# Seven block products over pairs of f tiles for the first matmul of the MLP, in the last two units

## The chip, the cores and the metric

The kernel runs on one core of one Trainium2 chip. The metric is the device time of one execution in microseconds (us). Five engines work side by side, each through its own queue in program order: TensorE (PE in the profile, its weight loads PEld), VectorE (DVE), ScalarE (ACT), GpSimd (POOL), and SyncE (SP), whose queue issues the DMA transfers. They meet through semaphores only. Matmuls write to PSUM, eight banks of 512 fp32 columns in each of 128 partitions; all else lies in SBUF or in DRAM.

## The reference

Two layers of each of two kinds in turn, on 2048 tokens of 1024 channels, in fp32: A, a gated long convolution on the normalized input, and B, an MLP with a squared ReLU.

```
x = x + A(layernorm(x)); x = x + B(layernorm(x)); x = x + A(layernorm(x)); x = x + B(layernorm(x))
B(x): h = x @ w1 + b1            # 1024 -> 3584
      h = max(h, 0) ** 2
      out = h @ w2 + b2          # 3584 -> 1024
```

Both layers of a kind use the same weights, and the convolution of A doesn't depend on x (only its gate does).

## The kernel before

**Units.** The MLP is computed for 512 tokens at a time: two layers of four blocks make eight units, run one after the other in the order of ORDER. What the convolution needs is computed beside units 0 to 4 on GpSimd and VectorE. Before a unit, its tokens are gated, normalized, turned on TensorE (transposes) and split into two tiles xh and xl.

**Three matmuls for one.** Every fp32 product is three matmuls on halves, hi x hi, hi x lo and lo x hi (mm3, lines 338 to 340): a number is cast to a shorter form by ScalarE (the high half), and what is left is the low half, a subtraction on VectorE. This holds for weights (line 1015 the cast, line 1023 the low half, in w_hi and w_lo) and for activations (1562, 1567).

**The first matmul (m1).** An f tile is 128 of the 3584 inner channels of the MLP; there are 28. For each f tile and each half kh of the 1024 input channels stands one step: a weight tile of 128 x 512 (four 128 x 128 blocks) against 512 tokens, 4 x 3 = 12 matmuls of 512 columns, gathered in one PSUM bank. Then relu_w makes the squared ReLU (lines 1559, 1560), splits it, and for the second tile of a pair forms four sums of blocks (1572 to 1575) and splits these as well (1579, 1583).

**The second matmul (w2) in the last three units.** Units 5, 6 and 7 (WINO) compute it as seven block products for eight, over pairs of f tiles, halves of the tokens and halves of the output columns. WORD gives the order of the seven blocks, WSUM where each is added. A step is one block of one pair: 2 x 3 = 6 matmuls of 512 columns. The 14 pairs are taken in four chunks, WCH = (3, 3, 4, 4): first all m1 steps of the chunk, then all its w2 steps, block by block, after which evict_w (line 1593) adds two PSUM banks to the accumulators.

**Weights.** All steps stand in one list, and each has a weight with a number in the same order. w_advance, called at each step, does three things ahead of the step: it loads raw weights up to 8 ahead (W_LOAD; w_load, lines 1004 and 1007, into a ring of 8 rows called wr), makes high halves up to 4 ahead (W_HI) and low halves up to 3 ahead (W_LO). Split pairs lie in a ring of six buffers (whl). Some weights are stored split at their first use (w_store) and later loaded as a pair of 512 KB, with no work on chip (split_kept, from_pair, line 1013); for the sums of w2's blocks ("t"), those are the weights of pairs 10 and up with a < 2, which are blocks 4 and 5. Everything is issued in one program order: an engine may run ahead of the step at which an instruction was issued, as far as data and buffers allow, but never past an earlier instruction in its own queue.

**What happens at a unit's start.** At its fifth step load_acc (line 1716) loads the four accumulators, at the seventh load_b2 (1721) loads the bias b2, at the eleventh add_b2 (1725) adds it on GpSimd:

```
b2_at = (7, 11) if u in WINO else (12, 16)
lag.at(b2_at[0], load_b2, bst)
lag.at(b2_at[1], add_b2, bst, accs)
```

lag is a list of things due so many steps later; it is emptied at the beginning of a step, ahead of w_advance. The block results of the unit before are stored by store_w (line 1600), on the same SP queue.

**Preparation.** In unit 5 and 6, prep_w readies the next unit from 90 steps before the end: early combines and takes statistics, late normalizes (847), turns (856) and splits (862, 864) one tile of 128 tokens after the other.

## Time and profile before

| | |
|---|---|
| median of 3 runs | 2715.45 us (2715.27 to 2721.26) |
| the profiled execution | 2718.27 us, its span 2716.5 us |
| mean granted TensorE clock | 0.996 |
| PE busy | 98% of the span |
| DVE, ACT, POOL busy | 73%, 41%, 31% of the span |
| unit 6, unit 7 from their first matmul | at 2125.25 and 2419.63 us |

A group line gives source line, engine, operation, tiles (out<-in), shapes, count, then busy us and mean ns of one, then the idle time of the engine just before, and what ended it. A timeline line gives start, duration, engine, line, operation, tiles and count, and in brackets the idle time before it and what released it. A line of a table by stretches gives the stretch and its length, then busy us and instructions of PE, PEld, DVE, ACT and POOL, the granted TensorE clock, the share of the DMA engines, and GB/s. Ends of matmuls are modelled, and matmuls overlap, so a pitch is read from starts.

### The profile page before, as it was taken

The page shows a single profiled execution, that of the slowest core. Times are in us where ns is not written, and L with a number is a line of the kernel's source. Part 1 is how long each engine was busy: PE and PEld are TensorE (multiplying, and loading weights), DVE is VectorE, ACT ScalarE, POOL GpSimd, SP SyncE. Part 2 cuts the span into 40 slices and gives each one's busy share as a digit, 9 for nine tenths or more (in the row PEclk, how much of TensorE's full clock was granted, in tenths as well). Part 3 has the DMA queues.
Part 4 walks back from the last instruction along what each step waited for, and adds up shares of the span by engine and source line. Part 5 has one row for each costly group of instructions (what it writes and reads, how often), then busy time and mean ns, then how long its engine had stood idle before and what let it go on. Part 6 is the DMA issues. An engine that isn't in the chain of part 4 may idle for free.

```text
span 2716.5 us, 36547 instructions
## 1 busy us (share of the span) xinstructions
PE 2660.4 (98%) x12568; PEld 2227.2 (82%) x12568; DVE 1984.6 (73%) x3042; ACT 1114.5 (41%) x1912; POOL 848.3 (31%) x520
## 2 busy tenths in 40 slices
PE   8999899999999999999999999999999999999998
PEld 7888787888888888888888888887888788878887
DVE  7878888788987878778677655367786666656554
ACT  4354344434444323442234322244455544444443
POOL 2336565445532745236552554001000100000000
PEclk9999999999999999999999999999999999999999
DMA  8889898689999898888977786798888766685555
GB/s 260 266 299 316 279 312 291 224 308 381 327 299 332 297 339 276 284 327 292 352 262 269 285 322 221 256 306 292 303 288 309 259 213 225 208 311 182 171 178 194
DMA packets 375898, 755.05 MB, mean 278 GB/s; under 512 B 43792, under 2 KB 159136, under 8 KB 375712
## 3 DMA queue, kind: packets, MB, share of 16 engines
q1 hardware_dynamic: 375712, 752.72, 80.9%
q8 instruction: 99, 1.62, 0.2%
q14 instruction: 87, 0.71, 0.1%
HBM read 602.63 MB, written 149.95 MB: 277 GB/s over the span
## 4 chain that ended last, share of the span: by engine, by line
PE 80%; DVE 7%; DMA 7%; issue 2%; POOL 2%; ACT 1%; SPq 1%; DVEq 0%; POOLq 0%; ACTq 0%
PE p L339 24%; PE p L340 24%; PE p L338 24%; PE p L1099 2%; DVE whl L1023 1%; DMA wr<-w 1%; DMA cg<-gd 1%; DMA whl<-wd_t 1%; PE pt L338 1%; PE pt L340 1%; PE pt L339 1%; POOL cp L528 1%; DVE sm L532 1%; DMA whl<-wd_m 1%; DMA yt<-yd 0%
## 5 line engine op out<-in xcount | busy, mean ns | idle before, releaser
L528 POOL TENSOR_TENSOR cp<-cx,cg 128x384 f32<-128x384 f32 (+5 forms) x288 | 545.2, 1906 | 567.5 <-DVE sm L532 376.6
L338 PE MATMUL p<-xh,whl 128*128 128x512 f32 (+1 forms) x1840 | 706.6, 384 | 0.6 <-DMA whl<-wd_m 0.6
L340 PE MATMUL p<-xh,whl 128*128 128x512 f32 (+1 forms) x1840 | 703.1, 382 | 0.8 <-POOL whl L1023 0.8
L339 PE MATMUL p<-xl,whl 128*128 128x512 f32 (+1 forms) x1840 | 703.1, 382 | 0.1
L1015 ACT CAST whl<-wr 128x512 fp32r<-128x512 f32 x637 | 385.4, 619 | 456.2 <-PE p L340 321.6
L1023 DVE TENSOR_TENSOR whl<-wr,whl 128x512 fp32r<-128x512 f32 x622 | 499.9, 826 | 71.2 <-ACT whl L1015 65.7
L338 PE MATMUL p<-whl,rh 128*128 128x512 f32 x1372 | 541.6, 395 | 4.2 <-ACT whl L1015 2.4
L339 PE MATMUL p<-whl,rh 128*128 128x512 f32 x1372 | 537.5, 392 | 5.5 <-DVE whl L1023 4.6
L340 PE MATMUL p<-whl,rl 128*128 128x512 f32 x1372 | 536.6, 391 | 0.0
L340 PEld LDWEIGHTS p<-xh,whl 128*128 128x128 f32 x1840 | 346.2, 188 | 68.4 <-POOL whl L1023 1.0
L338 PEld LDWEIGHTS p<-xh,whl 128*128 128x128 f32 x1840 | 346.6, 188 | 66.4 <-issue 1.1
L339 PEld LDWEIGHTS p<-xl,whl 128*128 128x128 f32 x1840 | 346.4, 188 | 65.8 <-DVE xl L1412 0.3
L1725 POOL TENSOR_TENSOR acc<-acc,px 128x1024 f32<-128x1024 f32 x32 | 84.8, 2681 | 738.2 <-DMA wr<-w 568.5
L339 PEld LDWEIGHTS p<-whl,rh 128*128 128x128 f32 x1372 | 259.0, 189 | 60.5 <-DVE whl L1023 7.5
L338 PEld LDWEIGHTS p<-whl,rh 128*128 128x128 f32 x1372 | 259.1, 189 | 58.1 <-ACT whl L1015 3.1
L340 PEld LDWEIGHTS p<-whl,rl 128*128 128x128 f32 x1372 | 258.9, 189 | 54.3
L1506 DVE TENSOR_TENSOR rl<-wr,rh 128x512 fp32r<-128x512 f32 x140 | 138.5, 990 | 183.7 <-ACT rh L1501 183.5
L532 DVE TENSOR_REDUCE sm<-cp 128x128 f32<-128x384 f32 (+5 forms) x288 | 249.5, 874 | 12.1 <-POOL cp L528 12.1
L1498 ACT ACTIVATE wr<-p,b1t 128x512 f32<-128x512 f32 x138 | 95.3, 690 | 367.2 <-PE p L340 366.4
L1567 DVE TENSOR_TENSOR rl<-wr,rh 128x256 fp32r<-128x256 f32 x84 | 51.0, 607 | 195.8 <-ACT rh L1562 195.6
L1593 DVE TENSOR_TENSOR acc<-p,acc 128x512 f32<-128x512 f32 x168 | 111.7, 687 | 67.7 <-PE p L340 67.6
L1605 DVE TENSOR_TENSOR acc<-p,acc 128x512 f32<-128x512 f32 x152 | 99.8, 686 | 82.2 <-PE p L340 82.2
(263 smaller groups left out, 3176.8 us busy)
## 6 DMA issues: line engine op xcount, KB each, us to landing
whl<-wd_m SPq DMA_DIRECT2D x379, 512.0 KB, 5.4
wr<-w SPq DMA_DIRECT2D x493, 256.0 KB, 5.3
wr<-td SPq DMA_DIRECT2D x152, 256.0 KB, 4.1
wd_m<-whl SPq DMA_DIRECT2D x70, 512.0 KB, 6.1
cx<-xd SPq DMA_DIRECT2D x48, 512.0 KB, 6.0
cg<-gd SPq DMA_DIRECT2D x48, 512.0 KB, 6.6
gd<-fg SPq DMA_DIRECT2D x72, 256.0 KB, 6.3
cx<-xd SPq DMA_DIRECT2D x48, 384.0 KB, 5.9
```

What stands on the lines that cost most here:

```text
L338: PE.matmul(o, lh, rh, start=start, stop=False, skip_group_check=skip)
L339: PE.matmul(o, lh, rl, start=False, stop=False, skip_group_check=skip)
L340: PE.matmul(o, ll, rh, start=False, stop=stop, skip_group_check=skip)
L528: G.tensor_mul(pr.rearrange("p c i -> p i c"), xt[:, 0:j + 1], gt[:, j::-1])
L532: V.tensor_reduce(sm[:, ty, jj], st["pr"], axis=AX.X, op=OP.add)
L1015: A.copy(t[:, 0], raws[n]["t"])
L1023: ENG[e[n % len(e)]].tensor_sub(t[:, 1], raws[n]["t"], t[:, 0].bitcast(F32))
L1498: A.activation(r, st["o"], AF.Relu, bias=b1t[:, st["f"]:st["f"] + 1])
L1506: V.tensor_sub(st["lo"], st["r"]["t"], st["hi"].bitcast(F32))
L1593: V.tensor_add(a, os[n], a)
L1605: V.tensor_add(accs[tt][:, d], o, accs[tt][:, d])
L1725: G.tensor_add(a, a, st["t"])
```

## The change

In units 6 and 7 (M1W) the first matmul is computed as seven block products instead of eight, too. For a pair of f tiles, the weight is cut into four blocks a11, a12, a21, a22 (second index: the half of the 1024 input channels; first index: the f tile), each 128 x 512, and the tokens into b11 to b22 (halves of input channels, halves of tokens). Sums of the weight blocks s1 to s4 are formed on GpSimd, in place or in rows of the ring (sums_a, sums_b), and sums of the token blocks once per unit in prep_w (first, second). Each product is a step "s1" of its own: 4 x 3 = 12 matmuls of 256 columns. Products are added up in two PSUM banks per pair; in between, m1_out copies a partial result out or across (three copies on ScalarE) and adds two on VectorE. The seven products of a pair are numbered like the blocks: 5, 1, 3, 2, 6 (with the first f tile then complete), 7, 4 (the second).

Beside it: the low halves of the products 3, 4 and 7 go to GpSimd; none of the product weights is kept split in DRAM; the order of the products of two pairs is interleaved, with the last two w2 steps of the chunk before and the first four of this one put in between; the chunks of units 6 and 7 are (2, 4, 4, 4); of the kept sums of w2's weights, blocks 5 and 6 are kept instead of 4 and 5; one square of the activation goes to another buffer (yt); two convolution tiles (sm, fk) become larger so that token pieces can lie in them; and the scratch for dynamic DMA is set to 1024.

```diff
+M1W = (6, 7)
+M1_KEY = {5: "s1", 1: "a11", 3: "s4", 2: "a12", 6: "s2", 4: "a22", 7: "s3"}
+M1_LO_G = (3, 4, 7)
-WCH = (3, 3, 4, 4)
+WCH, WCH_M1 = (3, 3, 4, 4), (2, 4, 4, 4)
...
+        for i, tt in enumerate((0, 2, 1, 3)):
+            for k, d in enumerate((0, 5)):
+                lag.at(W_PREP - W_LATE + 5 * i + d, late, tt, k)
+            for k in range(4 if tt > 1 else 3):
+                lag.at(W_PREP - W_LATE + 5 * i + 7 + k, second if tt > 1 else first, tt, k)
...
+            back = None
+            for a in pairs[::2]:
+                b = a + 1
+                if back:
+                    seq = [(5, a), (7, back[1]), (4, back[0]), (5, b), (1, a), (4, back[1]), (1, b)]
+                else:
+                    seq = [(5, a), tail, (5, b), tail, (1, a), (1, b)]
+                seq += [(3, a), (2, a), (6, a), (3, b), (2, b), (6, b), (7, a)]
+                back = a, b
+                if b == pairs[-1]:
+                    seq += [second, (7, b), second, (4, a), second if n > 2 else None, (4, b)]
...
-            return c >= T_KEPT and a < 2
+            return c >= T_KEPT and a in (1, 2)
...
+    def sums_a(g):
+        G.tensor_add(g["s1"]["t"], g["s3"]["t"], g["s1"]["t"])
+        del g["s1"]["late"]
+
+    def sums_b(g):
+        g["s2"], g["s4"] = row(), row()
+        s1, s2, s3, s4, a11, a12 = (g[x]["t"] for x in ("s1", "s2", "s3", "s4", "a11", "a12"))
+        G.tensor_sub(s2, s1, a11)
+        G.tensor_sub(s4, a12, s2)
+        G.tensor_sub(s3, a11, s3)
+        del g["s3"]["late"]
...
+        if j == 5:
+            get("s3", 1, 0, new("fx", 4))
+            get("s1", 1, 1, new("fg", 3))
+            pend.append((w + 2, 0, lambda: sums_a(g)))
+        elif j == 1:
+            get("a11", 0, 0, row())
+            get("a12", 0, 1, row())
+            pend.append((w + 2, 1, lambda: sums_b(g)))
+        elif j == 4:
+            get("a22", 1, 1, row())
...
+            if wsrc[n][0] == "s1" and wsrc[n][2] in M1_LO_G:
+                e = "G"
...
+    def m1_out(c, p, j, rp):
+        st0 = rs[c, 2 * p]
+        if j == 5:
+            st0["p5"] = ml.tile([P, XHALF], F32, name="p5", bufs=2)
+            A.copy(st0["p5"], st0["o"][:, XHALF:])
+        elif j == 1:
+            st1 = rs[c, 2 * p + 1] = {"o": pst(), "f": 2 * p + 1, "m1w": 1}
+            o = st1["o"][:, 0:XHALF]
...
+            A.copy(o, st0["o"][:, 0:XHALF])
+        elif j == 6:
+            u2 = ml.tile([P, XHALF], F32, name="u2", bufs=1)
+            A.copy(u2, rs[c, 2 * p + 1]["o"][:, 0:XHALF])
+            st0["u2"] = u2
+        elif j == 7:
+            o = rs[c, 2 * p + 1]["o"]
+            V.tensor_add(o[:, XHALF:], o[:, 0:XHALF], st0["p5"])
+        elif j == 4:
+            for kk in range(4):
+                lag.at(1 + kk, relu_w, rs[c, 2 * p + 1], kk, rp)
...
+        if k == "s1":
+            if a == 5:
+                rs[c, 2 * i] = {"o": ps1(), "f": 2 * i, "m1w": 1}
+            st0, st1 = rs[c, 2 * i], rs.get((c, 2 * i + 1))
+            o = st0["o"][:, 0:XHALF] if a in (1, 2) else st0["o"][:, XHALF:] if a in (5, 3) else st1["o"][:, 0:XHALF]
+            xs, ys = xT[a]
+            for kk in range(4):
+                t = slice(kk * P, (kk + 1) * P)
+                mm3(o, wh[:, t], wl[:, t], xs[:, kk], ys[:, kk], a == 5 and kk == 0, kk == 3, a != 5)
+            lag.at(1, m1_out, c, i, a, rp)
```

More of the change, by code (lines that the diff above doesn't have):

```diff
@@ L436, in fwd_g @@
         load_g(raw, sb, c)
[L437 removed]
+        kk = [mkfk([P, 2 * T])[:, 0:3 * BL] for _ in range(2)]
         for r in range(2):
@@ L902, in add_ahead @@
+            if c < len(chunks(u)) - 1:
+                second, tail = second[:-2], second[-2:]
+            for x in second:
+                m2(*x)
     def add_ahead(u, n):
@@ L975, in tile_h3_mlp, with room, rooms, run_pend @@
     tgen, made = [], set()
-    def room():
-        return len(ring) < RAWS or ring[-RAWS].get("freed", now[0]) < now[0] - 1
+    def room(n=1):
+        return all(len(ring) + k < RAWS or ring[k - RAWS].get("freed", now[0]) < now[0] - 1 for k in range(n))
+    pend = []
+    def rooms(w):
+        k, _, j, p = wsrc[w]
+        n = {1: 2, 4: 1}.get(j, 0) if k == "s1" else 1
+        return room(n + 2 * sum(x[0] <= w and x[1] for x in pend))
+    parts = {}
+    def sums_a(g):
[8 more added lines that the diff above has]
+        del g["s3"]["late"]
+    def run_pend(w):
+        while pend and pend[0][0] <= w:
+            pend.pop(0)[2]()
+    def load_s(w, j, p):
+        g = parts.setdefault(p, {})
+        def get(nm, f, kh, x):
+            g[nm] = x
+            SY.dma_start(x["t"], w1[2 * p + f, :, 4 * kh:4 * kh + 4])
+        def new(nm, m):
+            return {"t": cv.tile([P, 512], F32, name=nm, bufs=m), "late": True}
+        if j == 5:
[8 more added lines that the diff above has]
+            get("a22", 1, 1, row())
+            parts.pop(p)
+        while M1_KEY[j] not in g:
+            run_pend(pend[0][0])
+        raws[w] = g[M1_KEY[j]]
     def row():
@@ L1556, in relu_w @@
         if k == 0:
-            st["r"] = row()
+            st["r"] = {"t": ml.tile([P, 512], F32, name="yt", bufs=2)} if "m1w" in st and not e else row()
             r = st["r"]["t"]
```

161 lines of the change are left out of this document (135 added, 26 removed).

## The prediction

> **What bounds the kernel now.** I read the page first, for the engine that carries the span, then the table by stretches for the two units that the change touches, then single rows. On the page, the busy line and the line of the chain that ended last:
>
> ```profile
> PE 2660.4 (98%) x12568; PEld 2227.2 (82%) x12568; DVE 1984.6 (73%) x3042; ACT 1114.5 (41%) x1912; POOL 848.3 (31%) x520
> ...
> PE 80%; DVE 7%; DMA 7%; issue 2%; POOL 2%; ACT 1%; SPq 1%; DVEq 0%; POOLq 0%; ACTq 0%
> ```
>
> TensorE is the bound. The two last units, from the first matmul of each (its start is read from the timeline), columns as in the page's engines:
>
> ```profile
> 2125.25:2419.63 294.38, 291.26 (x1294) 239.40 (x1293) 190.01 (x339) 137.57 (x225) 10.45 (x4) 1.00 0.68 232
> 2419.63:2716.50 296.87, 287.84 (x1261) 235.76 (x1259) 161.24 (x261) 125.95 (x202) 10.36 (x4) 1.00 0.58 191
> ```
>
> The reader should see that TensorE is nearly full, VectorE is at 65% and 54%, ScalarE at 47% and 42%, and GpSimd does four instructions in each unit. So a shorter TensorE program is worth its saving only as long as VectorE, ScalarE and GpSimd deliver in time.
>
> **The matmuls.** Busy time overlaps between matmuls, so I price by starts: 24 matmuls 512 wide in a row, and 48 matmuls 256 wide in a row.
>
> ```profile
> 2419.63 0.39 PE L338 MATMUL p<-xh,whl 128*128 128x512 f32 x1
> ...
> 2424.84 0.39 PE L340 MATMUL p<-xh,whl 128*128 128x512 f32 x1
> ```
> ```profile
> 509.74 0.28 PE L338 MATMUL p<-xh,whl 128*128 128x256 f32 x1
> ...
> 515.38 0.28 PE L340 MATMUL p<-xh,whl 128*128 128x256 f32 x1
> ```
>
> That is 5.21 / 23 = 0.2267 us and 5.64 / 47 = 0.1200 us: half the width costs 53%, not 50%. Before, the first matmul of a unit is 56 steps of 12 matmuls, 672 x 0.2267 = 152.3 us. After, it is 14 pairs x 7 products x 4 inner tiles x 3 = 1176 x 0.1200 = 141.1 us. The saving is 11.2 us a unit, **-22.4** for two. The second matmul keeps its 588 instructions, 133.3 us. So even with no new wait only 0.8% is to be had.
>
> By the Trainium skill ("TensorE: Matmul & The Clock Gate", Back-to-back issue gap) a warm gap is N/2.4 + 2.5 ns, 109 and 216 ns; as an estimate from it the saving would be 16.6 us a unit, 33 in all. The trace disagrees, with 120 and 226.7 in unbroken runs, and it decides.
>
> **Kept weights.** In the last chunk the twelve consecutive weights of blocks 1, 5 and 4 come as kept pairs of 512 KB, one for each step of 6 x 0.2267 = 1.36 us, and TensorE waits for them. Unit 7 by single rows, unit 6 (from 2374 us) by group:
>
> ```profile
> 2687.56 0.47 PE L338 MATMUL p<-whl,cx 128*128 128x512 f32 x1 [1.78 <-DMA whl<-wd_t]
> 2690.16 0.51 PE L338 MATMUL p<-whl,cg 128*128 128x512 f32 x1 [0.98 <-DMA whl<-wd_t]
> 2692.11 0.50 PE L338 MATMUL p<-whl,cx 128*128 128x512 f32 x1 [0.28 <-DMA whl<-wd_t]
> 2694.71 0.50 PE L338 MATMUL p<-whl,cg 128*128 128x512 f32 x1 [0.94 <-DMA whl<-wd_t]
> ```
> ```profile
> L338 PE MATMUL p<-whl,cg 128*128 128x512 f32 x16 | 6.8, 422 | 1.3 <-DMA whl<-wd_t 1.3
> L338 PE MATMUL p<-whl,cx 128*128 128x512 f32 x16 | 6.4, 398 | 0.7 <-DMA whl<-wd_t 0.7
> ```
>
> The edit keeps blocks 5 and 6 instead of 4 and 5, so block 4's raw weights (256 KB, split on chip) break the run of twelve into eight and four. The waits are 4.0 and 2.0 us; between none and all of it goes, and I take half, **-3** (ends 0 and -6).
>
> **The start of a unit.** Here I expect the gain to go. The bias add is four GpSimd instructions, issued at the eleventh step of a unit. That number is unchanged, but a step of the first matmul shrinks from 12 x 0.2267 = 2.72 to 1.44 us, and now GpSimd's queue holds other work: the low halves of products 3, 4 and 7. Counting ticks, the adds go out at step 11 (product 7 of the first pair), and the low half for step 15 (product 4, issued three ahead, at step 12) stands right behind them. Before, nothing stood behind them. What times the adds is data:
>
> ```profile
> 2419.86 1.02 SPq L1600 DMA_DIRECT2D out<-acc  x2
> ...
> 2423.39 3.69 SPq L1716 DMA_DIRECT2D acc<-x  x4
> ...
> 2429.39 0.45 SPq L1721 DMA_DIRECT2D px<-b  x1
> ```
> ```profile
> 2438.40 10.36 POOL L1725 TENSOR_TENSOR acc<-acc,px 128x1024 f32<-128x1024 f32 x4 [283.65 <-DMA wr<-w]
> ```
>
> The last accumulators are stored at 0.2 us of the unit, reloaded from 3.8 to 7.4, the bias is asked for at 9.8, and the adds run from 18.8 to 29.1. On SP's queue after the change the bias load still stands behind the reload, but behind fewer weight loads: I put its issue at 7.7 and, with the same 9.0 us to the adds, the adds at 16.7 to 27.1. The low half follows at about 28.4 us. TensorE wants it after 12 products and 2 steps of the second matmul, 12 x 1.44 + 2 x 1.36 = 20.0 us, plus two matmuls, 0.24. The wait is 8.2 us in each unit, **+16.4**. Ends: if the bias landed 3.7 us earlier, 4.5 a unit; if at 18.8 as now, 10.3.
>
> After such a wait the granted clock falls. The nearest rows are those behind a 7.69 us wait earlier in the program:
>
> ```profile
> 299.76 1.10 PE L423 MATMUL pt<-ident,fx 128*128 128x128 f32 x4 [7.69 <-DVE fx L370]
> ...
> 305.36 0.52 PE L340 MATMUL p<-whl,rl 128*128 128x512 f32 x1
> ```
> ```profile
> 299.80:305.50 5.70, 5.70 (x16) 4.63 (x17) 5.39 (x10) 1.49 (x3) 3.54 (x3) 0.50 0.98 307
> ```
>
> 5.6 us at a granted 0.50 lose 2.8 us, **+5.6** for two (ends 0, if the wait is short, and 6). The Trainium skill (same page, What's actually happening) has the clock at half after an idle window of about 3.4 us until a busy window has passed, as an estimate 1.7 us lost for one window; the row shows a longer stretch than one, and I use the row.
>
> Then the first chunk, now of two pairs, ends: step 17 (block 1 of the second matmul, pair 1) follows directly on product 4 of pair 2. It needs pair 1's odd activation, split; the chain by single rows is
>
> ```profile
> 1925.39 0.69 ACT L1559 ACTIVATE wr<-p,b1t 128x512 f32<-128x512 f32 x1 [2.40 <-PE p L340]
> 1926.11 0.63 ACT L1560 ACTIVATE wr<-wr 128x512 f32<-128x512 f32 x1
> 1926.77 0.62 ACT L1562 CAST rh<-wr 128x512 fp32r<-128x512 f32 x1
> ```
> ```profile
> 1927.43 0.69 DVE L1567 TENSOR_TENSOR rl<-wr,rh 128x512 fp32r<-128x512 f32 x1 [1.29 <-ACT rh L1562]
> 1928.04 0.42 DVE L1572 TENSOR_TENSOR yl<-wr 128x256 f32<-128x256 f32 x1
> ...
> 1930.70 1.23 DVE L1583 TENSOR_TENSOR cp<-yl,cg 128x1024 fp32r<-128x1024 f32 x1
> ```
>
> From the first row to the end of the fourth are 2.7 us. At half clock one product (2.9 us) covers the first of these; then step 18 waits some 1.3 us for pair 2's chain, which queues behind pair 1's, and block 5 waits 1.1 us for the 1.23 us split of the sums: **+4.8** for two (ends 2 and 7; at full clock step 17 adds 1.3 us).
>
> **The shared port.** Per pair the new product loop adds to GpSimd four sums and three low halves of 128x512, to VectorE four low halves and two adds of 256 columns, to ScalarE seven casts and three copies of 256. They replace four weights a pair, of which some two and a half came from DRAM as kept pairs; the five loads of 256 KB that the products need are fewer bytes than before (1.3 against 1.7 MB a pair), so SP's queue and the DMA gain nothing and lose nothing here. Alone, GpSimd takes 1.26 us for one (two in 2.52) and VectorE 0.60 to 0.63 (three in 1.89); but where both have work with two inputs in SBUF, they take turns:
>
> ```profile
> 495.09 2.52 POOL L1023 TENSOR_TENSOR whl<-wr,whl 128x512 fp32r<-128x512 f32 x2 [2.62 <-ACT whl L1015]
> ...
> 541.00 1.73 POOL L1023 TENSOR_TENSOR whl<-wr,whl 128x512 fp32r<-128x512 f32 x1
> 542.69 1.76 POOL L528 TENSOR_TENSOR cp<-cx,cg 128x512 f32<-128x512 f32 x1
> 544.40 1.74 POOL L1023 TENSOR_TENSOR whl<-wr,whl 128x512 fp32r<-128x512 f32 x1
> ```
> ```profile
> 541.52 1.76 DVE L1023 TENSOR_TENSOR whl<-wr,whl 128x512 fp32r<-128x512 f32 x1
> 543.20 1.78 DVE L1506 TENSOR_TENSOR rl<-wr,rh 128x512 fp32r<-128x512 f32 x1
> ...
> 1940.64 1.89 DVE L1023 TENSOR_TENSOR whl<-wr,whl 128x512 fp32r<-128x512 f32 x3
> ```
>
> One of each every 1.70 us: nearly their sum, 1.86. A chunk of four pairs has 28 product steps and 28 of the second matmul, 28 x 1.44 + 28 x 1.36 = 78.4 us. GpSimd's 28 instructions at 1.10 to 1.26 are 31 to 35 us; VectorE's 16 + 28 low halves at 0.60 are 26.4, and its four activation chains, by the rows of the chain above some 0.4 + 0.6 + 1.4 + 1.2 = 3.6 each, 14. That is 71 to 75 us of a port in 78.4, and in the product half some 53 us for 40. Weights may run up to five steps (7 us) ahead of TensorE, which covers most of it; not all, and each chunk's bunch of sums (six in a row around the second pair of pairs) stands ahead of product 4's low half. I take 2 us for each of the six chunks, **+12**. If the lead covers everything, 0; if the 13 us come through less half of the lead, 8 a chunk and 48. ScalarE is no cover either. Two casts take 1.14 us there:
>
> ```profile
> 1927.30 1.14 ACT L1015 CAST whl<-wr 128x512 fp32r<-128x512 f32 x2
> ```
>
> so in the 20.2 us of two pairs' products it has 14 casts at 0.52, two odd and two even activations at some 1.9 and 1.7, two sum casts near 1.0 and six copies near 0.3: 18 us.
>
> **The preparation.** The turned tokens become fourteen pieces instead of eight, with eight subtractions: 14 more VectorE instructions of 0.60, 8.4 us in the last 25 steps of units 5 and 6, beside TensorE's 34. I take **+2** for both (ends 0 and 6). The larger sm and fk tiles and the smaller scratch move addresses only; one or two extra 256-wide matmuls are 0.1 us each.
>
> The old waits at a unit's start, caused by the same adds blocking VectorE, go, since the new ones take their place. In unit 7:
>
> ```profile
> L339 PE MATMUL p<-whl,rh 128*128 128x512 f32 x18 | 7.1, 396 | 0.6 <-DVE whl L1023 0.6
> ...
> L339 PE MATMUL p<-whl,cx 128*128 128x512 f32 x16 | 6.3, 397 | 0.5 <-DVE whl L1023 0.5
> ```
>
> 1.1 us a unit, **-2.2**. Sum: -22.4 - 3 + 16.4 + 5.6 + 4.8 + 12 + 2 - 2.2 = +13.2. The profiled execution took 2718.27 us (2716.5 of span and 1.8 around it), so 2731.5; it lies 2.8 above the median of 2715.45, which gives 2728.
>
> **The rivals.** *Faster: the bias adds hold nothing up.* If they were issued two steps later than I count, the low halves of both product 4s would stand ahead of them and GpSimd would have nothing due until the next chunk. The 22.0 us of wait and clock go: 2715.45 - 8.8 = 2707; if the lead covers the port as well, another 12, 2695. For it: before, GpSimd idles 283.65 us up to the adds, so room exists. Against: the count, and the data at 16 us. It decides once the adds end by 18.5 us. Chance 0.29, around 2700.
>
> *No measurable change.* 0.3%, 8 us, is about what a measurement of this kernel can tell. The bias lands 3.7 us earlier, the wait is 4.5 and the clock holds: -7.4 - 5.6, about 2716. Chance 0.25.
>
> *Much slower: the port becomes the bound.* At 8 us a chunk, 36 more, 2764. For it, 71 to 75 of 78.4; against it, the lead. Chance 0.11.
>
> *The change doesn't save what it says*, because 1176 weight loads for 1176 short matmuls don't keep 0.120. Weight loads are recorded at 188 ns:
>
> ```profile
> L340 PEld LDWEIGHTS p<-xh,whl 128*128 128x128 f32 x1840 | 346.2, 188 | 68.4 <-POOL whl L1023 1.0
> ```
>
> At that pitch a unit loses 69 us, 2850. The run of 48 speaks against it. Chance 0.02.
>
> **How the numbers follow.** My own sum has 0.33 (2724 to 2740). Slower is that with the last two, 0.46; same 0.25; faster 0.29. The range from 2698 to 2758 leaves out the lowest part of the faster case and the upper part of the port case, each about 0.1.
>
> **What would show it.** In the profile after: starts of 0.120 us in the products; one wait of 4 to 10 us at product 4 of the first pair in each unit, released by GpSimd, with the adds just before it on GpSimd and a granted clock near 0.5 behind it; VectorE low halves of over 1 us in the chunks. The prediction is wrong if that wait is missing, or if waits in the six chunks sum to over 25 us or to none.

## The result, and the profile after

The changed kernel is slower: a median of 2782.09 us over 4 runs (2779.64 to 2783.78) against 2717.54 us for the kernel before, 4 runs on the same chip. The ratio is 1.0235, with a 95% interval of 1.0218 to 1.0253. The prediction was 2728 us, with a range from 2698 to 2758. Its sign was right, its size was not: the loss is 64.6 us where the sum gave some 13.

The page of the changed kernel, the busy line and the line of the chain that ended last:

```profile
PE 2670.2 (96%) x13578; PEld 2270.7 (82%) x13578; DVE 2185.4 (79%) x3196; ACT 1231.7 (44%) x2174; POOL 1146.6 (41%) x716
...
PE 71%; DVE 11%; DMA 7%; issue 4%; ACT 3%; POOL 3%; SPq 1%; DVEq 0%; POOLq 0%; ACTq 0%
```

TensorE's share of the chain fell from 80% to 71%, and VectorE's rose from 7% to 11%. GpSimd does 196 instructions and 298 us more. The table by stretches tells where the time lies. A unit is taken here from its first matmul to the first of the next, the last unit to the end of its last matmul. For unit 7 of the kernel before, and then for units 6 and 7 of the changed one (columns as in the prediction: PE, PEld, DVE, ACT and POOL busy, then granted clock, DMA share, GB/s):

```profile
2419.63:2712.60 292.97, 287.77 (x1261) 235.76 (x1259) 160.44 (x260) 125.95 (x202) 10.36 (x4) 1.00 0.58 192
```
```profile
2125.65:2466.28 340.63, 302.39 (x1799) 265.31 (x1798) 290.32 (x416) 196.55 (x357) 162.42 (x105) 0.94 0.56 185
2466.28:2773.92 307.64, 286.36 (x1765) 254.41 (x1763) 247.75 (x324) 176.79 (x318) 153.62 (x97) 0.98 0.50 164
```

Unit 6 took 294.4 us and takes 340.6, **46 us more**; unit 7 took 293.0 and takes 307.6, **14.7 more**. Unit 6 starts within 0.4 us of where it did, but only because unit 5 began 2.0 us earlier in this execution: unit 5 took 302.1 us in place of 299.6. In the twelve profiled kernels, this one and those below, in which unit 6 is written as products, unit 5 takes 301.2 to 306.5 us; in the kernel before, e1 and e8 it takes 296.8 to 299.6. (e11 has other work there.) So some 5 us more are lost in unit 5, where unit 6 is prepared; what loses them was not tested. Units 6 and 7 have the same products; what only unit 6 has is the preparation of the next unit.

The pitch is what was predicted. The first and the last of 98 starts in a row, 11.64 / 97 = 0.1200 us:

```profile
2529.76 0.28 PE L342 MATMUL p<-xh,whl 128*128 128x256 f32 x1
...
2541.40 0.28 PE L343 MATMUL pt<-xc,whl 128*128 128x256 f32 x1
```

So a unit's matmuls are 1176 x 0.1200 + 588 x 0.2267 = 274.4 us, and unit 6 has 3.5 more of transposes. What stands above that, by chunk (starts of the chunks read from the timeline):

| above its matmuls, us | chunk 1 | chunk 2 | chunk 3 | chunk 4 | sum |
|---|---|---|---|---|---|
| unit 6 | 17.7 | 8.1 | 15.7 | 21.4 | 62.9 |
| unit 7 | 17.8 | 4.7 | 4.2 | 6.2 | 32.9 |

The starts of the units are alike in length. Chunks 3 and 4 of unit 6, in which unit 7 is prepared, lose 27 us more than those of unit 7.

**The start of a unit.** The rows of unit 7 around the predicted wait, TensorE's, then GpSimd's, then VectorE's:

```profile
2496.73 0.58 PE L344 MATMUL pt<-xh,whl 128*128 128x256 f32 x1 [5.23 <-POOL whl L1199]
```
```profile
2485.01 9.99 POOL L1944 TENSOR_TENSOR acc<-acc,px 128x1024 f32<-128x1024 f32 x4 [3.35 <-DMA wr<-w]
2494.96 3.40 POOL L1199 TENSOR_TENSOR whl<-wr,whl 128x512 fp32r<-128x512 f32 x2
```
```profile
2490.27 2.53 DVE L1199 TENSOR_TENSOR whl<-wr,whl 128x512 fp32r<-128x512 f32 x1
2492.72 1.27 DVE L1812 TENSOR_TENSOR acc<-p,acc 128x512 f32<-128x512 f32 x2
2493.92 4.99 DVE L1199 TENSOR_TENSOR whl<-wr,whl 128x512 fp32r<-128x512 f32 x3
```

In unit 7 the wait is where it was forecast: the four bias adds (L1944), right behind them the low half (L1199) of product 4, and TensorE idle 5.23 us until it is there. One thing was not forecast. While the adds run, a low half on VectorE takes 2.53 us in place of 0.6, as long as one 1024-wide add. The accumulator sums between them, which read PSUM, keep their 0.64 us each.

In unit 6 the forecast wait is missing. The adds start at the same 18.7 us of the unit, but TensorE is held up before it comes to product 4, at two second-matmul steps: 1.92 us for a cast of the activation, then 1.91 us for its low half, 256 columns wide, which takes VectorE 2.61 us beside the adds in place of 0.42. TensorE's, GpSimd's and VectorE's rows:

```profile
2154.74 0.80 PE L344 MATMUL p<-whl,rl 128*128 128x512 f32 x1 [1.91 <-DVE rl L1743]
```
```profile
2144.38 10.03 POOL L1944 TENSOR_TENSOR acc<-acc,px 128x1024 f32<-128x1024 f32 x4
```
```profile
2152.08 2.61 DVE L1743 TENSOR_TENSOR rl<-yt,rh 128x256 fp32r<-128x256 f32 x1 [1.52 <-ACT rh L1738]
```

Product 4 then starts at 2156.62 us without a wait.

**The preparation.** The longest wait of the changed units stands in chunk 4 of unit 6. VectorE, ScalarE and TensorE there:

```profile
2384.10 1.44 DVE L817 SCALAR_TENSOR_TENSOR px<-px,mv 128x512 f32<-128x512 f32 x1
2385.58 1.67 DVE L818 SCALAR_TENSOR_TENSOR px<-px,rs 128x512 f32<-128x512 f32 x1
2387.17 1.75 DVE L817 SCALAR_TENSOR_TENSOR px<-px,mv 128x512 f32<-128x512 f32 x1
2388.95 1.63 DVE L818 SCALAR_TENSOR_TENSOR px<-px,rs 128x512 f32<-128x512 f32 x1
...
2391.11 1.27 DVE L703 BATCH_NORM_STATS2 st<-px 128x6 f32<-128x512 f32 x2
```
```profile
2392.66 0.29 ACT L711 ACTIVATE sd<-mv,epst 128x1 f32<-128x1 f32 x1 [9.99 <-DVE mv L704]
```
```profile
2395.68 0.58 PE L342 MATMUL p<-xh,whl 128*128 128x256 f32 x1 [7.97 <-ACT p L1771]
```

The early stage of the preparation combines the residual of one tile of 128 tokens in four VectorE instructions (0.75 us each where nothing else holds the port), takes statistics, and asks ScalarE for a square root. While GpSimd forms sums and low halves, each of the four takes up to 1.75 us. (In the bursts of the other three tiles GpSimd is mostly idle, and ten of the twelve take 0.75.) The square root stands in ScalarE's queue from 2382.7 on and waits 9.99 us for the statistics. Behind it stand the casts of weights and the copy of product 5 out of PSUM (L1771), and so TensorE waits 7.97 us. Counted by instructions, that is at product 1 of the last pair; a second wait, 3.60 us, follows at product 7 of the same pair. (The expectations below call the two, by a miscount, the first and the sixth product of the last chunk.)

Chunk 3 loses its 15.7 us in another way. Two of the bursts stand there, GpSimd does nothing from 2313.6 to 2350.2 us, and TensorE waits at second-matmul steps for VectorE's low halves of weights, 5.9 us in five waits, the longest of which is

```profile
2334.80 0.50 PE L343 MATMUL p<-whl,cx 128*128 128x512 f32 x1 [2.20 <-DVE whl L1199]
```

### The profile page after: what moved, and what is told of

The parts are those of the page before. It is cut to its first block, busy times and chain, and to the rows that moved or that the text cites. A ratio compares the mean times of both kernels' runs of the same rounds, so it can differ in the third digit from the quotient of the medians.

```text
span 2777.9 us, 39498 instructions
## 1 busy us (share of the span) xinstructions
PE 2670.2 (96%) x13578; PEld 2270.7 (82%) x13578; DVE 2185.4 (79%) x3196; ACT 1231.7 (44%) x2174; POOL 1146.6 (41%) x716
## 3 DMA queue, kind: packets, MB, share of 16 engines
q8 instruction: 107, 1.75, 0.3%
## 4 chain that ended last, share of the span: by engine, by line
PE 71%; DVE 11%; DMA 7%; issue 4%; ACT 3%; POOL 3%; SPq 1%; DVEq 0%; POOLq 0%; ACTq 0%
PE p L344 21%; PE p L343 21%; PE p L342 21%; DVE whl L1199 2%; PE p L1275 2%; DMA wr<-w 2%; PE pt L344 2%; PE pt L342 1%; PE pt L343 1%; DVE rl L1743 1%; DMA wr<-td 1%; DMA whl<-wd_m 1%; POOL cp L532 1%; ACT whl L1189 1%; POOL whl L1199 1%
## 5 line engine op out<-in xcount | busy, mean ns | idle before, releaser
L1199 DVE TENSOR_TENSOR whl<-wr,whl 128x512 fp32r<-128x512 f32 x664 | 605.3, 932 | 64.2 <-ACT whl L1189 56.5
L342 PE MATMUL p<-xh,whl 128*128 128x512 f32 (+1 forms) x1728 | 629.3, 364 | 11.4 <-ACT p L1771 8.0
L344 PE MATMUL p<-xh,whl 128*128 128x512 f32 (+1 forms) x1728 | 626.5, 363 | 10.6 <-POOL whl L1199 6.3
L343 PE MATMUL p<-xl,whl 128*128 128x512 f32 (+1 forms) x1728 | 625.2, 362 | 0.1
L1189 ACT CAST whl<-wr 128x512 fp32r<-128x512 f32 x735 | 441.1, 619 | 403.0 <-PE p L344 297.4
L342 PE MATMUL p<-whl,rh 128*128 128x512 f32 x1372 | 543.3, 396 | 10.5 <-ACT rh L1738 5.5
L344 PEld LDWEIGHTS p<-xh,whl 128*128 128x128 f32 x1728 | 327.7, 190 | 63.4 <-POOL whl L1199 7.5
L342 PEld LDWEIGHTS p<-xh,whl 128*128 128x128 f32 x1728 | 328.1, 190 | 61.4 <-ACT p L1771 8.2
L343 PEld LDWEIGHTS p<-xl,whl 128*128 128x128 f32 x1728 | 327.9, 190 | 48.4 <-DVE xl L1588 0.3
L344 PEld LDWEIGHTS p<-whl,rl 128*128 128x128 f32 x1372 | 259.1, 189 | 60.3 <-DVE rl L1743 6.2
L1682 DVE TENSOR_TENSOR rl<-wr,rh 128x512 fp32r<-128x512 f32 x140 | 144.4, 1032 | 181.0 <-ACT rh L1677 180.8
L536 DVE TENSOR_REDUCE sm<-cp 128x128 f32<-128x384 f32 (+5 forms) x288 | 249.3, 873 | 10.5 <-POOL cp L532 10.5
L1108 POOL TENSOR_TENSOR fg<-fx,fg 128x512 f32<-128x512 f32 x28 | 40.7, 1457 | 445.9 <-DMA fg<-w 445.9
L1824 DVE TENSOR_TENSOR acc<-p,acc 128x512 f32<-128x512 f32 x152 | 100.0, 686 | 81.3 <-PE p L344 81.3
L1199 POOL TENSOR_TENSOR whl<-wr,whl 128x512 fp32r<-128x512 f32 x71 | 107.0, 1513 | 126.2 <-ACT whl L1189 101.6
L1944 POOL TENSOR_TENSOR acc<-acc,px 128x1024 f32<-128x1024 f32 x32 | 84.3, 2666 | 174.2 <-DMA px<-b 170.9
```

The costliest lines, as they stand in the source:

```text
L342: PE.matmul(o, lh, rh, start=start, stop=False, skip_group_check=skip)
L343: PE.matmul(o, lh, rl, start=False, stop=False, skip_group_check=skip)
L344: PE.matmul(o, ll, rh, start=False, stop=stop, skip_group_check=skip)
L536: V.tensor_reduce(sm[:, ty, jj], st["pr"], axis=AX.X, op=OP.add)
L1189: A.copy(t[:, 0], raws[n]["t"])
L1199: ENG[e[n % len(e)]].tensor_sub(t[:, 1], raws[n]["t"], t[:, 0].bitcast(F32))
```

## The experiments

For all of them, the lengths of units 6 and 7 in the profiled execution, the median, and the ratio with its interval to the kernel before, which was run again beside each group of runs (medians from 2715.5 to 2718.1 us). A length is that of one execution, and a difference between two medians of different groups carries some 2 us of doubt:

| run | unit 6 | unit 7 | median us | ratio |
|---|---|---|---|---|
| before | 294.4 | 293.0 | 2717.54 | |
| changed | 340.6 | 307.6 | 2782.09 | 1.0235 [1.0218, 1.0253] |
| e1 unit 7 alone | 294.9 | 307.0 | 2730.16 | 1.0048 [1.0031, 1.0064] |
| e2 bias adds later | 337.9 | 306.5 | 2781.84 | 1.0245 [1.0230, 1.0260] |
| e3 early stage in second-matmul steps | 332.9 | 305.9 | 2774.05 | 1.0214 [1.0199, 1.0229] |
| e4 square root later | 335.1 | 308.1 | 2777.94 | 1.0228 [1.0213, 1.0243] |
| e5 no bias adds | 333.4 | 297.2 | 2763.79 | 1.0171 [1.0157, 1.0185] |
| e6 no sums | 315.1 | 292.3 | 2739.63 | 1.0084 [1.0070, 1.0098] |
| e7 low halves on VectorE | 329.7 | 298.8 | 2757.52 | 1.0145 [1.0129, 1.0160] |
| e8 before, kept weights alone | 291.9 | 289.7 | 2710.79 | 0.9976 [0.9967, 0.9984] |
| e9 e5, e6 and e7 together | 307.5 | 282.3 | 2725.74 | 1.0028 [1.0017, 1.0039] |
| e10 unit 6 alone | 335.6 | 289.7 | 2761.56 | 1.0162 [1.0149, 1.0176] |
| e11 unit 7, sums made ahead | 304.2 | 288.7 | 2737.92 | 1.0079 [1.0066, 1.0091] |
| e12 e3 and e4 together | 330.9 | 307.0 | 2774.94 | 1.0208 [1.0193, 1.0224] |
| e13 no combines | 321.8 | 308.3 | 2764.71 | 1.0171 [1.0154, 1.0187] |
| e14 all moves | 326.5 | 294.6 | 2757.31 | 1.0145 [1.0127, 1.0162] |

### Which unit pays

e1 writes unit 7 alone as products, e10 unit 6 alone.

```
-M1W = (6, 7)
+M1W = (7,)     # e1
+M1W = (6,)     # e10
```

> Product form in unit 7 alone; unit 6 is written as before, so that unit 7's preparation (its form with seven pieces) stands in a unit with the old first matmul. Unit 6 lost 46 us to the kernel before and unit 7 some 15 us. Theory P (what makes unit 6 dear is the preparation of unit 7 meeting product steps, some 30 us): unit 6 is back at about 296 us, unit 7 costs its 15 us, total 2717.5 + 15 to 18 = 2731 to 2737. Theory Q (the seven-piece form of the preparation is dear wherever it stands): unit 6 stays above 310 us and the total is 2745 or more. Theory S (each unit in product form costs the same, half of 65 each): 2750.

> Product form in unit 6 alone: unit 7 and so its preparation are written as before, but that preparation stands in a product unit. In the changed kernel unit 6 lost 46 us, unit 7 (no preparation beside it) 14.6. Theory P1 (what is dear is the early stage, which is the same in both kernels: combines on the shared port, the square root in ScalarE's order): unit 6 stays 35 to 46 us longer than before, total 2750 to 2763. Theory P2 (what is dear is the new late stage: seven pieces, their differences and casts): unit 6 is 15 to 22 us longer, total 2731 to 2740.

The unit rows of e1:

```profile
2122.87:2417.78 294.91, 291.69 (x1294) 239.16 (x1293) 200.23 (x352) 145.14 (x240) 17.80 (x10) 1.00 0.68 233
2417.78:2724.74 306.96, 288.05 (x1767) 255.54 (x1765) 246.24 (x324) 176.72 (x318) 155.22 (x97) 0.98 0.49 164
```

Unit 6 is back at 294.9 us although unit 7's preparation in its new form, with seven pieces, stands in it. So that form costs 0.5 us beside the old first matmul there; theories Q and S fall, and the total, 2730.2, is a little under what P expected. In e10 unit 6 stays at 335.6 us, 41 above before, with a preparation written as before:

```profile
2132.97:2468.52 335.55, 297.64 (x1799) 263.33 (x1798) 276.06 (x403) 188.22 (x341) 151.19 (x96) 0.95 0.56 187
```

That is 5.1 us less than with the new form, by one execution of each; the medians differ by 20.5 us, of which unit 7's products are 18.0, and leave 2.5 for it. So P1 holds: neither the new form nor the products alone make unit 6 dear, but the old preparation beside the products. Unit 7's 307.6 and 3.5 of transposes make 311.1; unit 6 takes 340.6, so the preparation costs 29.5 us there.

### The bias adds

e2 moves the adds behind the low halves of both product 4s, e5 leaves them and the load of the bias out (no code shown).

```
-b2_at = (7, 11) if u in WINO else (12, 16)
+b2_at = (7, 20 if u in M1W else 11) if u in WINO else (12, 16)    # e2
```

> The changed kernel with the adds of the MLP's output bias (and with them the place where they stand in GpSimd's order) at the 20th step of units 6 and 7 in place of the 11th, behind the low halves of product 4 of the first pairs. Theory B (these adds stand ahead of the low half that TensorE needs): the wait of 5.4 us in unit 7 before product 4 and its counterparts in unit 6 go, and the total falls by 8 to 14 us, to 2768 to 2774. Theory S (the unit's start is bound by the sums and low halves on the shared GpSimd and VectorE port, the adds only come on top): the total falls by under 4 us.

The total did not move. GpSimd, VectorE and TensorE in unit 7 of e2:

```profile
2492.73 10.66 POOL L1944 TENSOR_TENSOR acc<-acc,px 128x1024 f32<-128x1024 f32 x4 [1.90 <-DVE acc L1812]
```
```profile
2493.17 8.02 DVE L1199 TENSOR_TENSOR whl<-wr,whl 128x512 fp32r<-128x512 f32 x3
2501.12 2.82 DVE L1743 TENSOR_TENSOR rl<-wr,rh 128x512 fp32r<-128x512 f32 x1
```
```profile
2503.99 0.79 PE L344 MATMUL p<-whl,rl 128*128 128x512 f32 x1 [7.37 <-DVE rl L1743]
```

The wait left product 4 and came back, 7.37 us long, at the second matmul. Four adds of 2.67 us let through four VectorE instructions, 8.02 / 3 = 2.67 us each, which alone take 0.67: VectorE gets one instruction for each one of GpSimd, however long that one is. The low half of the activation (rl), last of the four, is what TensorE waits for. So the order on GpSimd's queue, which the prediction named, only chose who waits. Unit 6 of the changed kernel, above, says the same.

By the Trainium skill ("SBUF — State Buffer", SBUF: two separate sides), GpSimd and VectorE share one pair of ports, taken as an exclusive lock for a whole instruction, by VectorE's when it has two inputs in SBUF. The rows agree: 2.67 us beside a 2.67 us add, and 0.64 for the sums that read PSUM.

> The changed kernel without the adds of the MLP's output bias (and without that row's load) in units 6 and 7; the bias is then missing from those units' outputs. The last run moved these adds and the total did not change: the wait left product 4 and came back at the second matmul behind VectorE's low half of a ReLU block, while VectorE's four two-input operations beside the four adds took 2.7 us each. Theory A (each 1024-wide add holds the port that VectorE shares with GpSimd for its whole length, so its price follows it to wherever it is put): without it 5 to 8 us go in each unit, total 2766 to 2772. Theory N (the unit's start is bound by the sums and low halves in any case, the adds lie beside them): under 3 us in total, 2777 to 2782.

Without the adds 18.3 us go, 7.2 in unit 6 and 10.5 in unit 7; that is theory A, and a little more than it said. The two runs together: the price follows the adds.

### The sums, the low halves, and all three at once

e6 takes the sums' place by loads; e7 puts the low halves on VectorE; e9 is e5, e6 and e7 in one.

```
-G.tensor_sub(s2, s1, a11)        # and the three others      e6
+SY.dma_start(g["s2"]["t"], w1[0, :, 0:4])    # and one for s4
-M1_LO_G = (3, 4, 7)
+M1_LO_G = ()                     # e7
```

> The changed kernel with the 56 sums of weight blocks per unit left out on GpSimd: the operand tiles take their place by loads (two more of 256 KB for each pair), so that the products are of wrong weights. GpSimd keeps its low halves. It prices the sums: 56 of them at 1.28 us alone, some 72 us of GpSimd time per unit. Theory W (the port shared by VectorE and GpSimd sets the pace of the chunks and of the units' starts; its demand in unit 7 is some 130 us of GpSimd and 150 of VectorE against a unit of 307): without the sums the two units lose 40 us or more, total 2730 to 2742. Theory L (the chunks' small losses are latencies of chains and of half clock): 10 to 20 us less, 2762 to 2772.

> The changed kernel with the low halves of products 3, 4 and 7 on VectorE in place of GpSimd (42 in each unit; 1.28 us each on GpSimd and 0.67 on VectorE where alone). Port demand of unit 7 falls from about 280 to 255 us, VectorE's own work rises to about 233. Theory W (the port): 8 to 25 us less, total 2757 to 2772. Theory V (VectorE in its own order becomes the bound and the preparation of unit 7 suffers most): 0 to 15 us more, 2782 to 2797.

> Three of the removals at once, in both units: no sums on GpSimd (loads in their place, so the products are of wrong weights), no bias adds (missing from the output), all low halves on VectorE; GpSimd then does nothing in the two units, and the port that it shares with VectorE is never held against VectorE. Singly they gave 42, 18 and 24 us. Theory W (the shared port is the whole of unit 7's loss): unit 7 comes to 277 to 283 us (274.4 is its matmuls alone); unit 6 keeps what its preparation costs beside the port, so that it comes to 295 to 305 us, total 2700 to 2712. Theory L (much of the loss is the latency of chains, and the three removals overlap): unit 7 stays at 288 us or more, total 2722 or more.

Units 6 and 7 of e6, of e7 and of e9:

```profile
2126.33:2441.44 315.11, 291.53 (x1800) 258.82 (x1798) 244.04 (x416) 195.48 (x357) 70.30 (x46) 0.97 0.66 224
2441.44:2733.73 292.29, 281.01 (x1765) 252.38 (x1763) 199.50 (x322) 177.34 (x319) 70.50 (x46) 0.99 0.59 196
```
```profile
2129.72:2459.38 329.66, 299.12 (x1799) 262.50 (x1798) 296.62 (x458) 196.26 (x358) 103.00 (x63) 0.96 0.57 191
2459.38:2758.20 298.82, 285.38 (x1765) 253.50 (x1763) 257.44 (x366) 176.05 (x318) 92.50 (x55) 0.98 0.50 169
```
```profile
2129.69:2437.14 307.45, 290.31 (x1800) 258.05 (x1798) 250.68 (x458) 195.56 (x357) 0.00 (x0) 0.98 0.69 228
2437.14:2719.42 282.28, 278.14 (x1765) 250.20 (x1763) 209.65 (x364) 177.17 (x319) 0.00 (x0) 1.00 0.61 201
```

Without the sums 42.5 us go, as theory W said. In unit 7 VectorE has the same work (322 instructions against 324) and is busy 199.5 us in place of 247.8: 48 us of its recorded time were waits for GpSimd. With the low halves on VectorE 24.6 us go, just inside W's bounds; in unit 7 it does 42 instructions more and is busy only 10 us longer. With GpSimd idle unit 7 comes to 282.3, 7.9 above its matmuls, and at a clock of 1.00. So what GpSimd does in unit 7 is 25 of the 33 us that it stands above its matmuls, as theory W has it: the start of unit 7 now stands 3.7 us above its matmuls in place of 17.8, chunks 2 and 3 stand 1.1 each in place of 4.7 and 4.2. The three removals overlap: together they give 56.4 us, singly 85. The total of e9, 2725.7, is W's no more but lies where theory L had it: unit 6 is 307.5, above the 295 to 305 that was expected (and in the profiled execution it began 4.4 us later than in the kernel before). 282.3 + 3.5 leaves 21.7 us for the preparation, even with the port free.

### The preparation

e3 places the early stage among second-matmul steps, e4 delays the square root, e12 does both, e13 leaves the combines out (unit 7's tokens then lack their first normalization and residual).

```
-lag.at(W_PREP - W_EARLY[tt] + d, early, tt, k)
+lag.at(W_PREP - ((86, 79, 72, 65) if (l, b) == ORDER[7] else W_EARLY)[tt] + d, early, tt, k)  # e3, e12
-for k, d in enumerate((0, 4, 5, 7)):
+for k, d in enumerate((0, 4, 5, 7, 13, 15)):   # e4, e12: k = 4 is rstd_a, k = 5 rstd_b
-combine(st["x"], st.pop("y"), mv[:, tt, 0:1], r[:, tt:tt + 1])
+y = st.pop("y")                                # e13; combine only if (l, b) != ORDER[7]
```

> The changed kernel with the early stage of unit 7's preparation (residual combines, statistics, square root) at 86, 79, 72 and 65 steps before the end of unit 6, so that tiles 1 to 3 stand among the third chunk's second-matmul steps, none among the last chunk's products. Theory P (this stage among products, where VectorE's combines share the port with GpSimd's sums, and the square root stands ahead of the casts on ScalarE, is where 20 of the 46 us go): the wait of 8 us at 2387 us goes, unit 6 shortens by 10 to 18 us, total 2764 to 2772. Theory C (the port is full anyway, the work only moves): under 4 us less, 2778 to 2782.

> The changed kernel with the square root of each preparation tile issued eight steps later, the rest of the early stage where it was: ScalarE then does not stand in its order behind VectorE's statistics. If ScalarE's place in the order is what turns VectorE's delay into a stall (10 us of waiting at the one square root of tile 3), the wait of 8 us before the product at 2395.7 us falls below 3 us and the total by 6 to 12 us, to 2770 to 2776. If VectorE's own lateness is what the products wait for, the stall stays and the total changes by under 3 us.

> The changed kernel with both moves of unit 7's preparation at once: its early stage at 86, 79, 72 and 65 steps before the end of unit 6, and the square root eight steps later than the statistics. Singly they gave 8 and 4 us. If they are two delays in one chain (VectorE's burst of combines, and ScalarE standing behind it), moving the burst leaves little for the second, and the total is 2770 to 2774; if each has its own stall, 2764 to 2769.

> The changed kernel without the residual combines of unit 7's preparation (the four two-input operations on each of its four tiles; the first normalisation and the residual of unit 7's tokens are thus left out, the statistics and square roots stay). With GpSimd idle (run e9) unit 6 still stood 25 us above unit 7, with waits of 5.4 us at two square roots while VectorE went through four combines of 0.75 us and the statistics. Theory D (the burst on VectorE, which stretches to 10 us where GpSimd holds the port, is what the preparation costs): the wait of 8 us at the first product of the last chunk and the one of 3.8 us at its sixth go, unit 6 loses 12 to 25 us, total 2756 to 2769. Theory H (the cost is that ScalarE's and VectorE's orders are shared at all, statistics and casts included): 3 to 10 us, 2771 to 2778.

e4, whose square root no longer stands ahead, still has both waits in chunk 4:

```profile
2390.94 0.58 PE L344 MATMUL p<-xh,whl 128*128 128x256 f32 x1 [3.34 <-DVE whl L1201]
...
2412.29 0.58 PE L342 MATMUL pt<-xc,whl 128*128 128x256 f32 x1 [5.26 <-ACT u L1783]
```

The first, now at the third matmul of product 1, is released by VectorE's low half behind the combines, 3.34 us in place of 7.97; the second grew from 3.60 to 5.26. The total fell by 4.2 us, between the two cases: ScalarE's place in the order lengthens the wait, but VectorE is late itself. e3 gained 8.0 us, 7.7 in unit 6, between its two cases as well: part of the burst's price goes with it to the second-matmul steps. e12 gained no more than e3 and lies just above the 2770 to 2774 us of one chain, which speaks for one chain and not two. e13 gained 17.4 us, and unit 6 alone is 18.9 shorter:

```profile
2130.37:2452.14 321.77, 293.44 (x1800) 258.89 (x1799) 277.19 (x400) 196.65 (x357) 165.51 (x104) 0.98 0.59 196
```

The wait for that copy out of PSUM is 0.66 us there, and the one at product 7 is 0.74:

```profile
2386.41 0.39 PE L342 MATMUL p<-xh,whl 128*128 128x256 f32 x1 [0.66 <-ACT p L1773]
...
2402.34 0.39 PE L342 MATMUL pt<-xc,whl 128*128 128x256 f32 x1 [0.74 <-ACT u L1783]
```

This is theory D: of the 29.5 us, the 16 combines are 18.9 (7.5 of it in chunk 3, 10.9 in chunk 4), and the new late stage 2.5 to 5.1 (e10), if the two do not overlap. The other 5 to 8 are not accounted for.

With GpSimd idle (e9) the same burst still costs a wait, without any stretching. VectorE, ScalarE, and TensorE at the same product 1 of the last pair:

```profile
2362.57 0.75 DVE L817 SCALAR_TENSOR_TENSOR px<-px,mv 128x512 f32<-128x512 f32 x1
...
2364.80 0.75 DVE L818 SCALAR_TENSOR_TENSOR px<-px,rs 128x512 f32<-128x512 f32 x1
```
```profile
2367.63 0.29 ACT L711 ACTIVATE sd<-mv,epst 128x1 f32<-128x1 f32 x1 [5.38 <-DVE mv L704]
```
```profile
2370.66 0.58 PE L342 MATMUL p<-xh,whl 128*128 128x256 f32 x1 [3.31 <-ACT p L1768]
```

### Versions meant to be faster

e8 is the kernel before with one line of the change.

```
-return c >= T_KEPT and a < 2
+return c >= T_KEPT and a in (1, 2)
```

> The kernel before, with the one change of the kept weights alone: of each late pair's combined blocks the second and third in place of the first and second are stored as pairs and loaded again in the last unit. I put this term at 3 us less for both units. If it is a gain by itself, the total falls by 1 to 3 us; if it only moves the waits, it is within 1 us of the kernel before.

It is 5.9 us faster than the kernel before, about twice the 1 to 3 us expected. The group rows for 2680 to 2700 us, where the kernel before had 2.1 and 1.9 us of waits for kept pairs in the same two groups:

```profile
L338 PE MATMUL p<-whl,cx 128*128 128x512 f32 x14 | 5.6, 398 | 0.8 <-DMA whl<-wd_t 0.8
L338 PE MATMUL p<-whl,cg 128*128 128x512 f32 x14 | 5.5, 396 | 0.3 <-DMA whl<-wd_t 0.3
```

e11 writes unit 7 alone as products and makes its sums ahead, on GpSimd in units 5 and 6; e14 keeps the sums where they are and makes all the other moves, those of e3 and e4 included.

```
-M1W = (6, 7)
+M1W = (7,)                       # e11 alone
-M1_LO_G = (3, 4, 7)
+M1_LO_G = ()                     # both
+G.tensor_add(t["a22"], t["a21"], t["a22"])       # e11: four such for each pair in units 5 and 6
+SY.dma_start(SD[p][:, n], t[nm])                 # e11: stored, and loaded in unit 7
+lag.at(20 + 3 * kk, add_b2_half, bst, accs, kk)  # both: eight halves, on GpSimd in e11, VectorE in e14
```

> A version meant to be faster: product form in unit 7 alone, its 56 sums of weight blocks made once on GpSimd during units 5 and 6 (GpSimd is idle there, 10 us busy in each) and kept in DRAM, so that every operand is one load; all low halves on VectorE; the bias adds as eight halves from the 20th step on, three steps apart. Unit 7 stood at 307 us (product form), 292 without sums, and the other two gave 9 and 10 us of unit 7; with no overlap between them it would be 275, so 278 to 285 us. The sums cost unit 6 and the end of unit 5 some 72 us of GpSimd time on the shared port and 100 GB/s more for a unit that moves 232. If that is hidden to within 5 us, the total is 2701 to 2710; if the port or the DMA queues make unit 6 pay, 2712 to 2722.

> The changed kernel with all that the runs found and that leaves the result whole: low halves of every product on VectorE (24 us), the early stage among the second matmul's steps and the square root late (8 and 4 us), and the bias adds as eight halves on VectorE, from the 20th step on, three steps apart (without the adds: 18 us). If they add up, less a few us for VectorE's added work, 2726 to 2735, still above the kernel before; if VectorE becomes the bound (some 240 us of its own work in unit 7, more in unit 6), 2736 to 2750.

Units 5, 6 and 7 of e11, and two of its groups of waits in units 5 and 6 (engine, line, releaser, then us in total, times, longest):

```profile
1825.60:2139.06 313.46, 299.99 (x1303) 243.68 (x1301) 235.44 (x427) 141.69 (x233) 39.63 (x24) 0.98 0.91 322
2139.06:2443.22 304.16, 295.26 (x1292) 239.73 (x1293) 217.94 (x351) 144.85 (x239) 61.31 (x40) 0.99 0.82 287
2443.22:2731.88 288.66, 280.80 (x1767) 251.60 (x1765) 215.79 (x364) 177.59 (x319) 13.30 (x8) 0.99 0.65 203
```
```profile
PE p L343 <- DVE whl L1236: 11.2, 11, 2.2
...
PE p L342 <- DMA whl<-wd_m: 8.2, 3, 3.1
```

Unit 7 is 18 us shorter than in e1 (288.7, above the 278 to 285 expected), but units 5 and 6 pay: unit 6 starts 13.8 us later than in the kernel before and is 9.8 longer. Waits for kept pairs (0.6 us in e8) and for VectorE's low halves (5.6 in e8) both grew. That is a miss, by 16 us over the worse of the two cases expected.

e14 came to the same total as e7 alone:

```profile
2127.24:2453.75 326.51, 292.75 (x1800) 255.18 (x1798) 293.32 (x466) 197.00 (x360) 98.35 (x61) 0.99 0.59 194
2453.75:2748.37 294.62, 283.62 (x1765) 251.97 (x1763) 251.39 (x374) 176.35 (x318) 83.93 (x50) 0.99 0.52 171
```

VectorE is busy 293 of 326 us in unit 6. The early stage's move gave 8 us in e3, and leaving out the bias adds gave 18 in e5; beside low halves that all stand on VectorE, that move and the adds as halves on VectorE gave nothing measurable. Which wait took the place of each was not followed. It is worse than both cases expected.

## Why the prediction was wrong

**The matmuls (-22.4): right.** The pitch is 0.1200 us, and in e9, with nothing holding the port, unit 7 is 10.7 us shorter than before, against 11.2 predicted.

**Kept weights (-3): right.** Waits for kept pairs in units 6 and 7 were 2.0 + 4.0 = 6.0 us before and are 0.6 + 2.2 = 2.8 in the changed kernel. Alone the line is worth 5.9 us (e8).

**The bias adds (+16.4) and the clock behind them (+5.6): the size right, the mechanism half.** Without the adds 18.3 us go. In unit 7 the wait was at the product and the engine named, 5.23 us instead of 8.2, because TensorE came to it 25.2 us into the unit and not 20.2, and the low half was there at 30.4 and not 28.4. In unit 6 it is missing, which the prediction had named as a sign of being wrong. The step "stands right behind them" on GpSimd's queue is not what carries the price, as unit 6 and e2 show; what the adds do to VectorE is. The rival "the bias adds hold nothing up" fails for the same reason: nine steps later changed nothing.

**The granted clock (part of the terms above).** It is 0.94 in unit 6 and 0.98 in unit 7 instead of 1.00. At half clock matmuls start 0.212 and 0.427 us apart (256 and 512 columns); 113 and 37 of them in the two units lose some 18 us. It is spread over all the waits, and contained in the terms of each, where the prediction had it only behind two.

**The starts of the units: under-sized.** Predicted 8.2 + 2.8 + 2.4 = 13.4 us each, less 1.1 of old waits; measured 17.7 and 17.8 above the matmuls, of which the adds are 7 to 10. With GpSimd idle (e9) 4.0 and 3.7 are left.

**The shared port (+12, at 2 us a chunk): under-sized.** Chunk 2 of unit 6 lost 8.1, the three of unit 7 15.1, of which 2.2 are kept pairs: some 4 to 8 a chunk. With GpSimd idle (e9) the same four stand 1.1 to 2.0 above their matmuls, and e6 (42.5 us) shows the same: the lead of up to five steps did not cover it. Without the preparation it was within the ends of 0 and 48. The six chunks as they are stand 60.3 us above their matmuls, far beyond the 25 that the prediction gave as a sign of being wrong. The rival "the port becomes the bound", with 0.11 and 2764 us, was nearer than the forecast.

**The preparation (+2, ends 0 and 6): the step that failed.** It measured 29.5 us in unit 6, and unit 5, where unit 6 is prepared, is some 5 us longer. Of about 50 us by which the forecast fell short, this is the largest part. The prediction counted only what the edit adds, "14 more VectorE instructions", and e10 puts the price of that at 2.5 to 5.1. The early stage, which the edit leaves as it is, was priced at nothing; no cover was named for it. Its cover was the slack of VectorE and ScalarE beside the old first matmul (e1: 294.9 us with the same work). In unit 6 VectorE's recorded time goes from 190 to 290 us (waits for the port included). A burst of four combines then puts the low halves behind it late: at second-matmul steps in chunk 3, and in chunk 4, where GpSimd's sums stretch one burst from 3.0 us to 6.5, also ScalarE's casts and copies, which stand behind a square root that waits for it. That the port only adds to this is shown by e9: 21.7 us are left with GpSimd idle.

The sum of what was measured: units 6 and 7 stood 5.3 and 7.4 us above their matmuls before, 62.9 and 32.9 after, so +83.1, less 22.4, gives +60.7 for the two units; the profiled spans differ by 61.4, the medians by 64.6.

## What to carry to other kernels

When a change fills an engine, price again every piece of work that the edit does not touch but that runs beside it: what was free beside a VectorE busy 65% of the unit cost some 25 us beside one busy 85%. VectorE and GpSimd took turns by whole instructions here, so a long instruction on GpSimd cost VectorE its full length at both places where it was put, and moving it moved the wait. Before building on a large change, run its small parts alone: here the one line that chooses which weights are kept was the only gain.

## What the runs showed of the hardware that was not expected

VectorE and GpSimd alternate whole instructions. A 0.67 us low half took 2.53 and 2.67 us beside 1024-wide adds of 2.67, and the sums on VectorE that read one input from PSUM (0.64) kept their time in the same stretch. Two statistics, which have one input in SBUF, took their usual 1.27 us at 2188.16 us, beside a GpSimd low half of 1.36.

The granted clock fell after a short gap. TensorE idled 2.67 us in unit 6, its only wait in 10 us, ran 1.5 us, and then stood at half speed for 3.40 us. The wait, and the table by stretches before, in and after the slow one:

```profile
2135.78 0.39 PE L344 MATMUL p<-xh,whl 128*128 128x256 f32 x1 [2.67 <-POOL whl L1199]
```

```profile
2135.70:2137.20 1.50, 1.42 (x12) 1.42 (x13) 1.50 (x2) 0.00 (x0) 1.50 (x2) 1.00 0.95 374
2137.20:2140.60 3.40, 3.40 (x19) 3.40 (x18) 0.78 (x1) 0.62 (x1) 1.50 (x2) 0.50 1.04 364
2140.60:2142.00 1.40, 1.40 (x13) 1.40 (x13) 0.00 (x0) 0.36 (x2) 0.00 (x0) 0.98 0.99 274
```

By the Trainium skill ("TensorE: Matmul & The Clock Gate", What's actually happening) the half clock comes after at least one idle window of about 3.4 us. The length of the stretch agrees with such a window; the gap that led to it was shorter, and here the measurement decides.
